# A gated mix of 32-head attention and SwiGLU: K and Q fetched later in each step, one V tile inside the score loop, three gate buffers, an end tile by tile

## The chip, the cores and the metric

One NeuronCore of a Trainium2 chip runs the kernel. The metric is the device time of one execution in microseconds (us), the median over runs. The profile is of one execution on that core.

## The reference

The inputs are x (1, 2048, 512), wqkv (512, 1536), wo (512, 512), w1 and w3 (512, 1792), w2 (1792, 512) and gate_w (512), all float32.

```python
g = sigmoid((x * gate_w).sum(-1, keepdims=True))
q, k, v = split(x @ wqkv)                      # 32 heads of 16
o = softmax(q @ k.T * 16 ** -0.5) @ v          # every query sees every key
a = o @ wo
b = (silu(x @ w1) * (x @ w3)) @ w2
return g * a + (1 - g) * b
```

## The kernel before

**Sizes.** A token tile is 128 tokens (NT = 16), a token quarter 512 (NB = 4), a feature tile 128 (ND = 4 of the 512 features, NF = 14 of the 1792). Projections and products are done in three terms from a high and a low part of each operand (high times high, high times low, low times high), the names end in H/L or h/l.

**Opening.** x is turned and split (xH, xL), the first 128 features of q and k are projected (`project_qk`), and the 16 tiles of V (`sums_v`: 12 full matmuls each, from xH/xL and the split weights wv). The last three V tiles are summed before, and copied out of their banks behind, a branch on a flag (`row_maxima`, `tc.If`) that all engines pass; its body runs for other inputs only.

**The score loop.** Work is cut into 1024 units: (head pair j, half of the queries, key tile k, quarter of the half gq). A unit is one `score` (two 50-row matmuls side by side, then one exponential on ScalarE, L841, from a score bank S into a buffer p) and its share of `pv` (two units at a time, four 17-column products side by side, L821, into acc). 32 units make a step: one head pair against half of the queries, with K and Q in Kt[i], Qt[i], i = step % 2. `evac` stores acc at a step's end.

**An order string written by hand** sets what TensorE does: Q is a score, F a fill slot, P a `pv` call. `run(n)` is n scores and 3n - 3 fill slots, then n/2 P; the pattern `two` has 8 scores, 15 fill slots and two P groups. All of the rest of the kernel goes through the fill slots: `feed` keeps two lanes, each of which does one matmul on 64 rows (half the contraction) per slot, side by side. A block (a product with what is done at its end) takes, say, 12 slots on one lane and then 12 on the other, on one PSUM bank of three, with a tiny VectorE instruction (`tick`, L793) as handover; `pick` hands blocks out in the order of `blocks()` once a bank has rested.

**The blocks in order:** q and k of the remaining features (chunks 0 to 2; `qk_done` splits and stores to qH_d, qL_d, kH_d, kL_d); gate and up for the 14 feature tiles f and four quarters b (chunks 3 to 16; `gate_done` copies to gs, an exponential goes to a buffer `sg`, L460, a reciprocal in eight parts, L463, the product L481 with the up side, and the store of sg to h_d, L482); then h times w2 per token tile in three parts (`h_product`, `load_piece(t, q)` fetches pieces of h and splits them on POOL); then o times wo (`o_product`, `part_product`). w2 takes the place of x, quarter by quarter, once the last chunk is through with that quarter.

**Events by unit number.** At unit 6 of a step, `load_step` fetches K and Q of the next step: 14 transfers on SP's queue, which is worked off in order. `splits`, `soon`, `small`, `later`, `loads` and `stages` are lists from which one or more actions are taken at a score. `divide` normalises finished heads (from D_d, O_d to N_d) and `six_heads` those of the last step.

**Buffers.** Eight exponential buffers p0 to p7, and in the first 512 units four more: od, yy and two halves of bt. In wk lie p, u, od, yy, bt, wo2, wo3; slots `sg` and `gs` have two buffers, `raw` and `fr` three.

**The end.** After the last PV, what is left of the blocks is fed, the last two heads are normalised and turned back, the last feature tile of o (k = 3) is multiplied by wo for token tiles 8 to 14 and all four for tile 15, and each tile is mixed (`mix`, L650) and stored. Tiles 8 and 9, 10 and 11, 12 and 13 are done in pairs; 8 and 10 go over ScalarE (`scaled`, L940) and POOL (L941).

Of the kernel before, what the change touches and what calls it, by code (L numbers as in the profile page):

```python
# [17 lines left out]
P = 128  # L18
# [10 lines left out]
SCALE = DH ** -0.5  # L29
SAFE = 64.0  # L30


@with_exitstack
def gated_mix_kernel(ctx: ExitStack, tc: tile.TileContext, x, wqkv, wo, w1, w3, w2, gate_w, out):
# [28 lines left out]
    fw = ctx.enter_context(tc.tile_pool(name="fw", bufs=2, side="right"))  # L63
    fk = ctx.enter_context(tc.tile_pool(name="fk", bufs=2, side="right"))
    ph1 = ExitStack()
    p1 = ph1.enter_context(tc.tile_pool(name="p1", bufs=1, side="right"))
    wvp = ph1.enter_context(tc.tile_pool(name="wvp", bufs=1))

# [141 lines left out]
    def load_v():  # L210
        for k in range(ND):
            r = slot(("fh1", "fl1", "fh3", "fl3")[k], F32)
            nc.sync.dma_start(r, wqkv[P * k:P * k + P, 2 * D:3 * D])
            vh, vl = (wvp.tile([P, 512], F32R, name=f"v{n}{k}") for n in "hl")
            nc.gpsimd.tensor_copy(vh, r)
            nc.gpsimd.tensor_sub(vl, r, vh)
            wv.append((vh, vl))
# [193 lines left out]
    small = nc.values_load(flag, min_val=0, max_val=1)  # L411
    last_v = [sums_v(t) for t in range(NT - 3, NT)]
    row_maxima(small)
# [38 lines left out]
    def gate_done(f, b):  # L452
        def done(ps):
            gs = slot("gs", F32)
            nc.vector.tensor_copy(gs, ps)  # L455
            sg = slot("sg", F32)
            st = state[b] = dict(gs=gs, sg=sg, exp=False, up=None, gone=False, last=f == NF - 1 or f == NF - 2 and b > 1)

            def exp():
                nc.scalar.activation(sg, gs, AF.Exp, scale=-1.0)  # L460
# [73 lines left out]
    def load_wo(k):  # L534
        if k < 2:
            hi, lo = w2H[3][:, 2 + k, :], w2L[3][:, 2 + k, :]
        else:
            both = wk.tile([P, 2, 512], F32R, name=f"wo{k}")
# [68 lines left out]
    def divide(k, half):  # L607

        yield from reciprocals(k, half)
        for b in (2 * half, 2 * half + 1):  # L610
            for _ in range(5):
                yield
            if half == 0 and k < 3:
                o, r = slot("hx", F32), slot("gw", F32)
            else:
                both = wk.tile([P, 2, 512], F32, name="od")
                o, r = both[:, 0, :], both[:, 1, :]
# [11 lines left out]
    def load_bt(t):  # L629
        if t == 0:  # L630
            bt[-1] = wk.tile([P, 4, 512], F32, name="bt")
        bt[t] = bt[-1][:, t % 3, :]
        nc.sync.dma_start(bt[t], B_d[P * t:P * t + P, :])
# [61 lines left out]
    def six_heads():  # L695
# [8 lines left out]
        nc.sync.dma_start(rows(R_d), dd[rr])  # L704
        both = wk.tile([P, 2, 512], F32, name="od")
        pairs = [(both[:, 0, :], both[:, 1, :]), (slot("fr", F32), slot("sg", F32))]
# [7 lines left out]
        for b in (2, 3):  # L714
# [27 lines left out]
    NBLOCK = 8 * len(chunks) + 3 * NT + NT // 2 + NT // 2  # L742
    source = blocks()

    REST, GAP = 7, 6
    lanes, ready, over = [None, None], ([], []), []
    halves = [None, None]
    tick = const.tile([1, P], F32, name="tick")
# [6 lines left out]
    def pick(lane, rest, gap):  # L755
        if ready[lane] and (ready[lane][0]["since"] + gap <= clock or gap == 0):
            return ready[lane].pop(0)
        used = len(over) - 3
        if used < 0 or over[used] is not None and over[used] + rest <= clock:
            block, halves[lane] = halves[lane] or next(source, None), None  # L760
            if block:
                if type(block[1]) is tuple:
                    product, done, length = block
                    block, halves[1 - lane] = (product, done[0], length), (product, done[1], length)
                over.append(None)
                return dict(block=block, ps=bank(), id=len(over) - 1, n=0, turn=None, alone=halves[1 - lane] is not None or len(over) == NBLOCK)
        return None
# [60 lines left out]
    def score(j, half, k, gq):  # L828
# [7 lines left out]
        n = free.pop(0)  # L836
        if n in ("b0", "b1"):
            p = twin[:, 0:2, :] if n == "b0" else twin[:, 2:4, :]
        else:
            p = wk.tile([P, 2, 512], F32, name=f"p{n}" if type(n) is int else n)  # L840
        nc.scalar.activation(p, ps, AF.Exp, scale=SCALE)  # L841
# [13 lines left out]
    twin = wk.tile([P, 4, 512], F32, name="bt")  # L855

    units = iter([(j, half, k, gq) for half in range(2) for j in range(NPAIR) for k in range(NT) for gq in range(2)])
    pend, clock = [], 0
    for i, c in enumerate(order):
        clock += 1 if c != "P" else 4  # L860
        if c == "Q":
            step = issued // 32 + 1
            if issued % 32 == 6 and step < 2 * NPAIR:
                assert 8 * (ND - 1) - qk_left >= 8 * min(step // 4, ND - 1)
                load_step(step)
# [10 lines left out]
            if small or later and hurry:  # L876
                for _ in range(3 if hurry else 1 + (len(small) > (6 if len(over) < 8 * len(chunks) - 16 else 0))):
                    if small or later and hurry:
                        (small or later).pop(0)()
            if loads and (hurry or issued % 2 or len(over) > 8 * len(chunks) - 12):  # L880
                loads.pop(0)()
# [43 lines left out]
    project(last, 0, (1, 2))  # L925
    project(last, 1, (0, 1))
    rr = slice(PAD, P)
# [10 lines left out]
    def scaled(t):  # L938
        y = wk.tile([P, 512], F32, name=f"p{free[t // 2 - 3]}")
        nc.scalar.activation(y, banks[t], AF.Copy, scale=g[:, t:t + 1])  # L940
        nc.gpsimd.tensor_add(bt[t], bt[t], y)  # L941

    def store(t):
        nc.sync.dma_start(out[P * t:P * t + P, :], bt[t])

    banks[8], banks[9] = one_[:, 1, :], two_[:, 1, :]
    banks[10], banks[11] = bank(), bank()
    for two in ((8, 9), (10, 11), (12, 13), (14,), (15,)):
        if two[0] == 12:
            banks[12], banks[13], banks[14] = psum2()[:, 0, :], psum2()[:, 0, :], acc  # L950
        for terms in ((0, 1), (2,)):
            for t in two:
                project(t, k, terms)
        for t in two:
            if t in (8, 10):
                scaled(t)
            elif t < last:
                mix(t, banks[t], nc.scalar if t % 2 == 0 else nc.sync)
                if t in (9, 11):
                    store(t - 1)  # L960
            else:
                mix(t, banks[t], nc.scalar, slice(0, D // 2))
                mix(t, banks[t], nc.sync, slice(D // 2, D))

# [26 lines left out]
```

## Time and profile before

| what | value |
|---|---|
| median of 3 runs | 1421.45 us (1420.95 to 1421.45) |
| the profiled execution: time, span | 1420.64 us, 1418.8 us |
| busy: TensorE / ScalarE / VectorE / POOL | 1398.6 / 1034.0 / 483.9 / 327.8 us |
| granted TensorE clock, mean | 0.994 |
| moved by DMA | 141.03 MB, mean 99 GB/s |

In a row of the profile stand the line of the kernel, the engine, what was written from what, and how often; in brackets the engine's idle time just before and what ended it. PE is TensorE's matmuls, ACT ScalarE, DVE VectorE, POOL GpSimd; SPq and ACTq are the queues on which transfers are issued. The chain of waits lists the work that ended last in order of time (start, length, what). A table by stretch gives each engine's busy time, then the granted clock, the share of the DMA engines and GB/s.

### The profile page before, as it was taken

How to read it: one execution, taken by the hardware profiler on the slowest of the kernel's cores; microseconds unless marked ns; L12 is line 12 of the kernel's file. 1: busy time of each engine (PE TensorE's matmuls, PEld its weight loads, DVE VectorE, ACT ScalarE, POOL GpSimd, SP SyncE). 2: the span in 40 equal slices, each digit the busy share in tenths (PEclk: the TensorE clock that was granted, in tenths of full speed). 3: DMA queues.
4: the chain of work that ended last, by engine and by line, in shares of the span. 5: the costliest groups of instructions: out<-in, count | busy, mean ns of one | idle time of the engine just before them, and what ended most of it. 6: DMA issues, size and time to landing. Idle time of an engine off the chain costs nothing.

```text
span 1418.8 us, 29039 instructions
## 1 busy us (share of the span) xinstructions
PE 1398.6 (99%) x11497; PEld 835.1 (59%) x11497; DVE 483.9 (34%) x1083; ACT 1034.0 (73%) x1155; POOL 327.8 (23%) x366
## 2 busy tenths in 40 slices
PE   9999999999999999999998999899999999999998
PEld 8875656565656565656564655555555555555554
DVE  5511112554555554655563546210111100111113
ACT  4456767777877777777775777667788878887784
POOL 6114442101001110011101145322333232312312
PEclk9999999999999999999999999999999999999999
DMA  7654554343214333224333165413554543434632
GB/s 207 166 113 108 143 133 104 70 113 69 63 40 98 98 84 68 55 65 110 69 68 69 57 159 120 102 50 83 113 124 91 119 109 76 110 86 108 157 124 77
DMA packets 112479, 141.03 MB, mean 99 GB/s; under 512 B 16276, under 2 KB 70804, under 8 KB 109264
## 3 DMA queue, kind: packets, MB, share of 16 engines
q1 hardware_dynamic: 111616, 137.92, 40.4%
q8 instruction: 93, 1.52, 0.5%
q10 hardware_dynamic: 720, 1.18, 0.2%
q14 instruction: 50, 0.41, 0.1%
HBM read 90.43 MB, written 48.61 MB: 98 GB/s over the span
## 4 chain that ended last, share of the span: by engine, by line
PE 88%; issue 4%; DMA 2%; POOL 2%; SPq 1%; DVE 1%; ACT 1%; DVEq 0%; POOLq 0%; ACTq 0%
PE acc L821 30%; PE f L432 22%; PE S L834 17%; PE f L550 11%; PE f L638 2%; PE S L199 2%; PE f L645 1%; PE f L96 1%; PE f L98 1%; PE f L97 1%; DMA kH_d<-sg 1%; POOL gs L445 1%; DMA h_d<-sg 1%; SPq L270 1%; ACT p L841 1%
## 5 line engine op out<-in xcount | busy, mean ns | idle before, releaser
L841 ACT ACTIVATE p<-S 128x1024 f32<-128x1024 f32 x854 | 810.3, 1026 | 251.1 <-PE S L834 242.0
L834 PE MATMUL S<-Qt,Kt 50*128 50x512 f32 x2048 | 410.3, 407 | 6.1 <-ACT p L841 5.4
L821 PE MATMUL acc<-p,V 128*17 128x512 f32 x3416 | 401.5, 596 | 0.0
L834 PEld LDWEIGHTS S<-Qt,Kt 50*128 50x128 f32 x2048 | 188.3, 185 | 172.9 <-ACT p L841 82.8
L463 DVE RECIPROCAL sg<-sg 128x64 f32<-128x64 f32 x448 | 209.6, 517 | 61.1 <-issue 58.2
L432 PE MATMUL f<-xH,fl 64*128 64x512 f32 x1088 | 224.3, 397 | 0.5 <-DVE tick L793 0.3
L432 PE MATMUL f<-xL,fh 64*128 64x512 f32 x1088 | 222.4, 394 | 0.0
L821 PEld LDWEIGHTS acc<-p,V 128*17 128x17 f32 x3416 | 86.2, 97 | 231.1 <-issue 231.1
L432 PE MATMUL f<-xH,fh 64*128 64x512 f32 x1088 | 221.4, 390 | 0.3 <-DVE gs L455 0.3
L328 POOL CAST fh<-fr 128x512 fp32r<-128x512 f32 x34 | 21.3, 626 | 443.1 <-DMA fr<-in_B_w_dram 358.4
L432 PEld LDWEIGHTS f<-xH,fh 64*128 64x128 f32 x1088 | 108.8, 185 | 24.6 <-DVE gs L455 0.7
L432 PEld LDWEIGHTS f<-xH,fl 64*128 64x128 f32 x1088 | 109.0, 187 | 23.0 <-DVE tick L793 0.8
L432 PEld LDWEIGHTS f<-xL,fh 64*128 64x128 f32 x1088 | 109.0, 187 | 20.9
L793 DVE MEMSET tick<- 1x1 f32 x198 | 11.7, 59 | 306.3 <-PE f L550 181.0
L841 ACT ACTIVATE bt<-S 128x1024 f32<-128x1024 f32 x84 | 82.2, 1028 | 20.3 <-PE S L834 20.3
L841 ACT ACTIVATE od<-S 128x1024 f32<-128x1024 f32 x43 | 44.3, 1029 | 41.4 <-PE S L834 41.4
L550 PE MATMUL f<-xH,fh 64*128 64x512 f32 x208 | 58.3, 394 | 0.0
L550 PE MATMUL f<-xH,fr 64*128 64x512 f32 x160 | 52.0, 397 | 5.9 <-POOL fr L513 5.4
L550 PE MATMUL f<-xH,raw 64*128 64x512 f32 x192 | 57.7, 392 | 0.0
L455 DVE COPY gs<-f 128x512 f32<-128x512 f32 x56 | 38.1, 681 | 55.8 <-PE f L432 53.4
L803 DVE COPY u<-acc 128x512 f32<-128x512 f32 x31 | 21.4, 692 | 104.6 <-PE acc L821 97.1
L550 PE MATMUL f<-xL,fh 64*128 64x512 f32 x208 | 56.1, 392 | 0.0
(211 smaller groups left out, 1577.9 us busy)
## 6 DMA issues: line engine op xcount, KB each, us to landing
Kt<-kH_d SPq DMA_DIRECT2D x128, 128.0 KB
h_d<-sg SPq DMA_DIRECT2D x56, 256.0 KB
sg<-h_d SPq DMA_DIRECT2D x43, 256.0 KB
fr<-in_B_w_dram SPq DMA_DIRECT2D x42, 256.0 KB
Qt<-qH_d SPq DMA_DIRECT2D x128, 64.0 KB
Kt<-kL_d SPq DMA_DIRECT2D x64, 128.0 KB
Qt<-qL_d SPq DMA_DIRECT2D x64, 64.0 KB
b_d<-yy SPq DMA_DIRECT2D x16, 256.0 KB
```

The costliest lines, as they stand in the source:

```text
L96: nc.tensor.matmul(ps, sH, mH, start=first, stop=False)
L199: nc.tensor.matmul(ps[:, i, :], w[i][h][:, k, :], xs[b][:, k, :], start=n == 0, stop=n == len(order) - 1)
L328: nc.gpsimd.tensor_copy(hi, src)
L432: return nc.tensor.matmul(ps, w[i == 1][r, k, :], (xL if i == 2 else xH)[b][r, k, :], start=n == 0 and not second, stop=n == 3 * ND - 1 an ...
L455: nc.vector.tensor_copy(gs, ps)
L463: small.append(lambda q=q: nc.vector.reciprocal(sg[:, q:q + 64], sg[:, q:q + 64]))
L550: ins = nc.tensor.matmul(ps, hs[t][q][i == 1][r, P * o:P * o + P], (w2L if i == 2 else w2H)[q][r, o, :], start=n == 0 and not second, stop ...
L638: return nc.tensor.matmul(ps, ot[t][i == 1][r, P * k:P * k + P], wo_[k][i == 2][r, :], start=n == 0 and not second, stop=n == 3 * ND - 1 a ...
L803: nc.vector.tensor_copy(u, acc)
L821: nc.tensor.matmul(acc[r:r + DH + 1, :], V[:, k, 2 * j + h, :], p[:, h, :], start=k == 0, stop=k == NT - 1)
L834: nc.tensor.matmul(ps[:, h, :], Kt[i][r:r + 50, P * k:P * k + P], Qt[i][r:r + 50, t:t + 512], start=True, stop=True)
L841: nc.scalar.activation(p, ps, AF.Exp, scale=SCALE)
```

## The change

1. `EARLY = 15`: only V tiles 13 and 14 are summed before the loop; tile 15 is the first block of `blocks()`.
2. V's weights move to the pool wvp, kept to the end, as four tiles v0 to v3 of two halves. These are the four extra p buffers (`MORE`), free only when the first run's PV are issued, and later hold od (v2), the third and fourth part of wo and the first pieces of h (v0, v1), and two of the three bt buffers (v3).
3. A third `sg` buffer in wk serves every third gate.
4. `load_step` comes at unit 14 of a step, for units 608 to 639 at 18 of the step, from 640 on at 6.
5. The order string: the first step is 8, 12, 12 instead of 12, 10, 10; 20 run(8) instead of 18 and 43 `two` instead of 45.
6. The last two chunks go through quarters 0, 1, 2 of the last but one, then of the last, then quarter 3 of each, instead of 0 and 1, then 2, then 3.
7. Token tile 13's part of o, like 14's, is two half blocks on two banks without handover; near the end a bank rests 3 instead of 7.
8. The end goes tile by tile, all mixed on VectorE.

```diff
+EARLY = 15
+    wvp = ctx.enter_context(tc.tile_pool(name="wvp", bufs=1))
     p1 = ph1.enter_context(tc.tile_pool(name="p1", bufs=1, side="right"))
-    wvp = ph1.enter_context(tc.tile_pool(name="wvp", bufs=1))
...
-            vh, vl = (wvp.tile([P, 512], F32R, name=f"v{n}{k}") for n in "hl")
+            both = wvp.tile([P, 2, 512], F32R, name=f"v{k}")
+            vh, vl = both[:, 0, :], both[:, 1, :]
...
-    last_v = [sums_v(t) for t in range(NT - 3, NT)]
+    last_v = [sums_v(t) for t in range(13, EARLY)]
...
-            sg = slot("sg", F32)
+            sg = wk.tile([P, 512], F32, name="sg") if (NB * f + b) % 3 == 2 else slot("sg", F32)
...
-            both = wk.tile([P, 2, 512], F32R, name=f"wo{2 + q}")
+            both = wvp.tile([P, 2, 512], F32R, name=f"v{q}")
...
-        turns += [(last - i, b) for two in ((0, 1), (2,), (3,)) for i in (1, 0) for b in two]
+        turns += [(last - i, b) for some in ((0, 1, 2), (3,)) for i in (1, 0) for b in some]
+        for t in range(EARLY, NT):
+            yield v_product(t), v_done(t), 3 * ND
...
+    def v_product(t):
+        b, o = divmod(P * t, 512)
+        def product(ps, r, n, second):
+            k, i = divmod(n, 3)
+            return nc.tensor.matmul(ps, (xL if i == 1 else xH)[b][r, k, o:o + P], wv[k][i == 2][r, :],
+                                    start=n == 0 and not second, stop=n == 3 * ND - 1 and second)
+        return product
+
+    def v_done(t):
+        return lambda ps: nc.vector.tensor_copy(V[:, t, :, 0:DH], ps.rearrange("p (h d) -> p h d", d=DH))
...
-        for t in range(NT // 2, NT - 2):
+        for t in range(NT // 2, NT - 3):
             yield part_product(t, True), part_done(t), LATE
-        yield part_product(NT - 2, False), (part_done(NT - 2), part_done(NT - 2)), LATE
+        for t in (NT - 3, NT - 2):
+            yield part_product(t, False), (part_done(t), part_done(t)), LATE
...
-        if used < 0 or over[used] is not None and over[used] + rest <= clock:
+        if used < 0 or over[used] is not None and over[used] + (rest if len(over) < NBLOCK - 3 else 3) <= clock:
...
-    THIRDS, LONG, SHORT = 16, 18, 45
+    THIRDS, LONG, SHORT = 16, 20, 43
-    order = (run(12) + run(10) * 2) * THIRDS + run(8) * LONG + "QQ" + "F" * 7 + two * SHORT + "QFFF" * 5 + "QPPPP"
-    MORE = ["od", "yy", "b0", "b1"]
-    free = list(range(NP)) + MORE
+    order = run(8) + run(12) * 2 + (run(12) + run(10) * 2) * (THIRDS - 1) + run(8) * LONG + "QQ" + "F" * 7 + two * SHORT + "QFFF" * 5 + "QPPPP"
+    MORE = ["v0", "v1", "v2", "v3"]
+    free = list(range(NP))
...
-            if issued % 32 == 6 and step < 2 * NPAIR:
+            if issued % 32 == (14 if issued < 608 else 18 if issued < 640 else 6) and step < 2 * NPAIR:
...
+            if issued == 8 and not pend:
+                free += MORE
...
-    project(last, 1, (0, 1))
+    project(last, 1)
...
-    project(last, 1, (2,))
-    project(last, 2)
+    project(last, 2, (0, 1))
...
-    for two in ((8, 9), (10, 11), (12, 13), (14,), (15,)):
...
+    project(8, k, (0, 1))
+    project(last, 2, (2,))
+    project(8, k, (2,))
+    mix(8, banks[8])
+    for t in range(9, NT):
...
+        project(t, k)
+        if t < last:
+            mix(t, banks[t], nc.scalar if t % 2 else nc.sync)
```

More of the change, by code (lines that the diff above doesn't have):

```diff
@@ L537, in load_wo @@
         else:
-            both = wk.tile([P, 2, 512], F32R, name=f"wo{k}")
+            both = wvp.tile([P, 2, 512], F32R, name=f"v{k - 2}")
             hi, lo = both[:, 0, :], both[:, 1, :]
@@ L615, in divide @@
             else:
-                both = wk.tile([P, 2, 512], F32, name="od")
+                both = wvp.tile([P, 2, 512], F32, name="v2")
                 o, r = both[:, 0, :], both[:, 1, :]
@@ L630, in load_bt @@
         if t == 0:
-            bt[-1] = wk.tile([P, 4, 512], F32, name="bt")
-        bt[t] = bt[-1][:, t % 3, :]
+            both = wvp.tile([P, 2, 512], F32, name="v3")
+            bt[-3], bt[-2] = both[:, 0, :], both[:, 1, :]
+            bt[-1] = wk.tile([P, 512], F32, name="bt")[:]
+        bt[t] = bt[t - 3]
         nc.sync.dma_start(bt[t], B_d[P * t:P * t + P, :])
@@ L704, in six_heads @@
         nc.sync.dma_start(rows(R_d), dd[rr])
-        both = wk.tile([P, 2, 512], F32, name="od")
+        both = wvp.tile([P, 2, 512], F32, name="v2")
         pairs = [(both[:, 0, :], both[:, 1, :]), (slot("fr", F32), slot("sg", F32))]
@@ L736, in blocks @@
             yield o_product(t), o_done(t), 3 * ND
-        for t in range(NT // 2, NT - 2):
+        for t in range(NT // 2, NT - 3):
             yield part_product(t, True), part_done(t), LATE
-        yield part_product(NT - 2, False), (part_done(NT - 2), part_done(NT - 2)), LATE
+        for t in (NT - 3, NT - 2):
+            yield part_product(t, False), (part_done(t), part_done(t)), LATE
     LATE = 3 * (ND - 1)
-    NBLOCK = 8 * len(chunks) + 3 * NT + NT // 2 + NT // 2
+    FIRST = NT - EARLY + 8 * len(chunks)
+    NBLOCK = FIRST + 3 * NT + NT // 2 + NT // 2 + 1
     source = blocks()
@@ L746, in gated_mix_kernel @@
     lanes, ready, over = [None, None], ([], []), []
-    halves = [None, None]
+    halves = [[], []]
     tick = const.tile([1, P], F32, name="tick")
@@ L758, in pick @@
         used = len(over) - 3
-        if used < 0 or over[used] is not None and over[used] + rest <= clock:
-            block, halves[lane] = halves[lane] or next(source, None), None
+        if used < 0 or over[used] is not None and over[used] + (rest if len(over) < NBLOCK - 3 else 3) <= clock:
+            alone = bool(halves[lane])
+            block = halves[lane].pop(0) if alone else next(source, None)
             if block:
@@ L763, in pick @@
                     product, done, length = block
-                    block, halves[1 - lane] = (product, done[0], length), (product, done[1], length)
+                    block, alone = (product, done[0], length), True
+                    halves[1 - lane].append((product, done[1], length))
                 over.append(None)
-                return dict(block=block, ps=bank(), id=len(over) - 1, n=0, turn=None, alone=halves[1 - lane] is not None or len(over) == NBLOCK)
+                return dict(block=block, ps=bank(), id=len(over) - 1, n=0, turn=None, alone=alone)
         return None
@@ L836, in score @@
         n = free.pop(0)
[L837 to L840, printed above, removed]
+        p = (wk if type(n) is int else wvp).tile([P, 2, 512], F32, name=f"p{n}" if type(n) is int else n)
         nc.scalar.activation(p, ps, AF.Exp, scale=SCALE)
@@ L848, in gated_mix_kernel @@
     NP = 8
-    THIRDS, LONG, SHORT = 16, 18, 45
+    THIRDS, LONG, SHORT = 16, 20, 43
     run = lambda n: "QQFFFFFF" + "QFFF" * (n - 3) + "Q" + "P" * (n // 2)
     two = "QFFF" * 5 + "QPPQQPP"
-    order = (run(12) + run(10) * 2) * THIRDS + run(8) * LONG + "QQ" + "F" * 7 + two * SHORT + "QFFF" * 5 + "QPPPP"
-    MORE = ["od", "yy", "b0", "b1"]
-    free = list(range(NP)) + MORE
-    twin = wk.tile([P, 4, 512], F32, name="bt")
+    order = run(8) + run(12) * 2 + (run(12) + run(10) * 2) * (THIRDS - 1) + run(8) * LONG + "QQ" + "F" * 7 + two * SHORT + "QFFF" * 5 + "QPPPP"
+    MORE = ["v0", "v1", "v2", "v3"]
+    free = list(range(NP))
     units = iter([(j, half, k, gq) for half in range(2) for j in range(NPAIR) for k in range(NT) for gq in range(2)])
@@ L876, in gated_mix_kernel @@
             if small or later and hurry:
-                for _ in range(3 if hurry else 1 + (len(small) > (6 if len(over) < 8 * len(chunks) - 16 else 0))):
+                for _ in range(3 if hurry else 1 + (len(small) > (6 if len(over) < FIRST - 16 else 0))):
                     if small or later and hurry:
                         (small or later).pop(0)()
-            if loads and (hurry or issued % 2 or len(over) > 8 * len(chunks) - 12):
+            if loads and (hurry or issued % 2 or len(over) > FIRST - 12):
                 loads.pop(0)()
@@ L934, in gated_mix_kernel @@
         nc.vector.tensor_sub(Ol[k][rr, a, :], back[a][rr, :], Oh[k][rr, a, :])
-    project(last, 1, (2,))
-    project(last, 2)
[L938 to L944, printed above, removed]
+    project(last, 2, (0, 1))
     banks[8], banks[9] = one_[:, 1, :], two_[:, 1, :]
     banks[10], banks[11] = bank(), bank()
-    for two in ((8, 9), (10, 11), (12, 13), (14,), (15,)):
-        if two[0] == 12:
-            banks[12], banks[13], banks[14] = psum2()[:, 0, :], psum2()[:, 0, :], acc
[L951 to L963, printed above, removed]
+    project(8, k, (0, 1))
[3 more added lines that the diff above has]
+    for t in range(9, NT):
+        if t == 12:
+            banks[12], banks[13], banks[14] = psum2()[:, 0, :], psum2()[:, 0, :], acc
+        project(t, k)
+        if t < last:
+            mix(t, banks[t], nc.scalar if t % 2 else nc.sync)
+        else:
+            mix(t, banks[t], nc.scalar, slice(0, D // 2))
+            mix(t, banks[t], nc.sync, slice(D // 2, D))
 _INS = ['A_x', 'A_wqkv', 'A_wo', 'B_w1', 'B_w3', 'B_w2', 'gate_w']
```

## The prediction

> **What bounds the kernel now.** I read the page first: the engine that is nearly always busy sets the time, if it is busy at full clock.
>
> ```profile
> PE 1398.6 (99%) x11497; PEld 835.1 (59%) x11497; DVE 483.9 (34%) x1083; ACT 1034.0 (73%) x1155; POOL 327.8 (23%) x366
> ```
>
> TensorE it is: only its work, its order and its stops count. The stops show in the chain of waits in order of time, where each run of scores and fill ends in one group of PV products (L821): the distance between two such groups is the length of a run.
>
> ```profile
> 220.28 5.28 PE acc L821 x48
> ...
> 262.67 5.27 PE acc L821 x48
> ...
> 757.99 4.42 PE acc L821 x40
> ...
> 787.50 3.56 PE acc L821 x32
> 798.00 3.56 PE acc L821 x32
> ...
> 903.28 3.56 PE acc L821 x32
> ...
> 933.55 3.56 PE acc L821 x32
> ...
> 1107.57 1.84 PE acc L821 x16
> ...
> 1117.00 1.84 PE acc L821 x16
> ```
>
> A step of 32 units (runs of 12, 10, 10) takes 42.39 us, run(8) 10.50, the pattern `two` (also 8 units) 9.43. Against that, 757.99 to 787.50 is 29.51, where two runs of 8 and the longer first PV group (4.42 - 3.56) make 21.86: **7.65 us lost**. 903.28 to 933.55 is 30.27 for two runs: **9.27 lost**. Then the rows of TensorE, ScalarE, SP's queue and the wait list, for what ended each stop:
>
> ```profile
> 780.11 0.79 PE L834 MATMUL S<-Qt,Kt 50*128 50x512 f32 x2 [5.12 <-ACT p L841]
> ```
> ```profile
> 778.51 0.63 ACT L460 ACTIVATE sg<-gs 128x512 f32<-128x512 f32 x1 [7.50 <-DMA h_d<-sg]
> ```
> ```profile
> 766.15 0.36 SPq L277 DMA_DIRECT2D Qt<-qH_d  x1
> ...
> 773.30 10.16 SPq L482 DMA_DIRECT2D h_d<-sg  x2
> ```
> ```profile
> 773.30 5.13 DMA h_d<-sg
> ```
> ```profile
> ACT sg L460 <- DMA h_d<-sg: 18.1, 4, 7.5
> ```
>
> First stop, read backwards: a score waits for a score bank, which ScalarE empties; ScalarE stands 7.50 us before a gate's exponential, whose `sg` buffer (two, in turn) is still being stored to h_d; that store came to the head of SP's queue at 773.30, behind the 14 transfers of the `load_step` begun at 766.15, and took 5.13. ScalarE waits so four times, 18.1 us in all; the other three cost TensorE little.
>
> ```profile
> 905.88 0.45 SPq L277 DMA_DIRECT2D Qt<-qH_d  x1
> ...
> 913.49 7.83 SPq L512 DMA_DIRECT2D sg<-h_d  x4
> ```
> ```profile
> 918.49 0.79 PE L550 MATMUL f<-xH,fr 64*128 64x512 f32 x1 [5.39 <-POOL fr L513]
> ```
>
> Second stop, same queue: the pieces of h for token tile 1 (`load_piece(1, 2)`, `(1, 3)`, into `fr`) sit behind a `load_step` that holds SP from 905.88 to 913.4; TensorE waits 5.39 for their split.
>
> **The change, part by part.** Its sum stands against this execution: 1418.8 us of span, 1420.64 of time, so 1.84 around the span; the median of the runs, 1421.45, is 0.8 above it.
>
> *Third `sg` buffer, `load_step` at unit 14.* A gate-up pair takes 24 fill slots; at 87 slots per 42.39 us that is 11.7, so the buffer written now was last taken two pairs ago (23.4 us), with three buffers 35.1. ScalarE was 7.50 short; 11.7 more leaves 4.2 over. The fetch still holds SP for 773.30 - 766.15 = 7.15 us, whatever its unit: moved from 6 to 14 it goes behind the qk stores, chunk weights, h stores and (unit 12) `dd` loads issued in between, and ahead of those after. At 14 it no longer follows the accumulator's eight stores directly. Queued behind it is now the h store of that moment, for which ScalarE waits two buffers later: covered by the 4.2. For the first stop I take -7.6 (bounds -7.6 and 0: no row shows three buffers; the nearest, the 7.50, is exceeded by 11.7). Small losses: 16 steps of 42.39 from the first score, 81.40 (row below), would end at 759.64, and the sixteenth ends at 757.99 + 4.42 = 762.41, 2.8 late. I take 1.5 of it as gone, the rest as the qk part's own, where `gs` and slot `sg` stay two (bounds 0 and -2.8).
>
> *Unit 18 for units 608 to 639.* I walked both order strings, counting slots. Before, the fetch stands at unit 614 and the pieces (1, 2), (1, 3) at 615 and 616. After, the pieces stand at 620 and 621, the fetch at 626; they are first used at slot 1711, unit 634, a run after they are asked for. The last product of the last chunk is 5 units later (619): its gate now ends inside the run of units 608 to 615, so its exponential comes at 616, not 608; its store feeds token tiles 12 to 15 alone. -9.3 (bounds -9.3, 0). What is late next: the last two pieces of w2 come at units 614 and 615 instead of 612 and 613, and are used from slot 1673, unit 619. One PV group, 3.56, lies between and covers the transfer. I put +0.5 there, from 0 to 3.6 (that cover gone). The fetch of step 20 keeps 14 units, 18 us at 10.50 per 8.
>
> *Order and V tile 15.*
>
> ```profile
> 80.06 0.39 PE L97 MATMUL f<-vl,xH 128*128 128x512 f32 x1
> 80.29 0.39 PE L98 MATMUL f<-vh,xL 128*128 128x512 f32 x1
> 81.40 0.93 PE L834 MATMUL S<-Qt,Kt 50*128 50x512 f32 x4 [0.72 <-DVE V L415]
> ```
> ```profile
> 73.76 0.55 SPq L282 DMA_DIRECT2D Qt<-m_d  x2
> 79.75 0.32 SPq L277 DMA_DIRECT2D Qt<-qH_d  x1
> ```
>
> Tile 15 was 12 full matmuls at a pitch of 0.23: 2.7 us. As a block it is 24 half matmuls, two side by side, 12 slots. Two `two` (15 slots each) become two run(8) (21 each), exactly those 12: 2 x (10.50 - 9.43) = +2.1. The first step's order 8, 12, 12 has the same number of runs and slots. In return the first score could come 2.7 earlier, at 78.7; but SP, which must pass the If too, issues nothing between 73.76 and 79.75. I take the first score at 80.1, -1.3 (bounds -2.7, 0; nearest is SP's row). [...] The buffers v0 to v3 hold V's weights until the block's last slot, 27; their first exponential is the ninth of the second run, near slot 48: no wait. The copy of V's tile on VectorE is the same copy, moved (34% busy). Without that cover a wait there would be one copy, below 1 us.
>
> *3 and 1 token quarters; buffers.* The same blocks in another order; w2's first pieces move from unit 560 to 574, the first pieces of h from 564 to 580, both far ahead of the first h product (slot 1633, unit 604): 0. `od`, `wo2`, `wo3` and most of `bt` move to v0 to v3 with the same lifetimes: 0. If this cover failed, it would be a stop as at 918.49.
>
> *End.*
>
> ```profile
> 1403.03 0.50 PE L645 MATMUL f<-wo,xL 64*128 64x512 f32 x1
> 1403.37 0.39 PE L645 MATMUL f<-wo,xH 64*128 64x512 f32 x1
> ```
> ```profile
> 1409.81 0.37 SPq L651 DMA_DIRECT2D out_dram<-xH  x1
> 1410.93 0.36 SPq L944 DMA_DIRECT2D out_dram<-xH  x1
> ```
> ```profile
> GB/s 0 0 0 0 0 0 0 191 410 355 210 0 200 410 364 383 401 337 392 346 419 364 382 401 346 392 410 346 373 373 364 341 355 328 132 0 0 0 0 0
> ```
>
> Tile 13 without turns saves a handover and adds one sum on VectorE, hidden in PV; by the slot count three fill slots are left behind the last PV group, two before: +0.3. Then the same matmuls, tile by tile. The last row is 1409 to 1418 in columns of 0.225 us: the first output tile flows for 0.7, then a hole of 0.4, since tiles 8 and 9, 10 and 11 are finished in pairs and two of them pass ScalarE and POOL; then the bus is full for 5 us to 1416.8. Tile by tile the first store leaves three matmuls (0.69) sooner and 0.3 later for the fill slot, near 1409.4, and each next 0.69 after it, which is what a tile takes on the bus: no hole, nothing heaped up, the end set by the last half tile's store, whose product comes as late as now. -1.0 (bounds -1.4, 0).
>
> **Sum:** -7.6 - 1.5 - 9.3 + 0.5 + 2.1 - 1.3 + 0.3 - 1.0 = -17.8; 1420.64 - 17.8 = 1402.8. The median stands up to 0.8 higher: I say **1403**.
>
> **Rivals.** *A, the second stop moves:* the last w2 or h pieces are late after all. For it: w2's last piece now queues behind an h piece on POOL, which splits in order. Against it: the half run and more between each asking and use. 3 to 9 of the 9.27 us back: 1406 to 1412. *B, the clock.*
>
> ```profile
> 772.85:787.50 14.65, 9.53 (x66) 7.12 (x66) 6.00 (x17) 7.29 (x8) 0.00 (x0) 0.77 0.36 65
> ```
>
> Around the first stop the granted clock averaged 0.77, and of the 7.65 lost only 5.12 were idle: 2.5 went to matmuls at the lower clock. Now TensorE idles before the first score from the end of tile 14, 81.40 - 2.7 - 0.7 = 78.0, to 80.1: 2.1 us where it was 0.72. If that lowers the clock: +2.5, 1405.5. [...] *C, the store still holds ScalarE* (fetch, stores and weights heaped at unit 14): the 7.6 stay: 1410.5. *D, slower:* K and Q come late. After unit 14, 18 of 32 units are left, 23.8 us; the fetch takes 7.2 to issue, and a transfer lands 5.13 later, so 11.5 are over. Only if the last landed 11.5 + 1 us late at each of some 19 step boundaries would the 18 us be eaten: above 1421.5. No wait for Kt is among the stops now. *E:* the stops have another cause: 1421.
>
> **How the numbers follow.** Forecast 0.70 (1399.5 to 1406), A 0.12, B 0.07, C 0.05, D 0.04, E 0.02. A change under 0.2% (2.8 us) is about what measuring this kernel can't tell from none: faster 0.94, same 0.02, slower 0.04. Low end, every bound at its best: -7.6 - 2.8 - 9.3 + 2.1 - 2.7 + 0.3 - 1.4 = -21.4, 1399.3. High end: into A, 1409, which leaves out half of A, C, D and E, under 2 in 10.
>
> **What would show it.** No row of L460 waiting for h_d longer than 1 us, 757.99 to 787.50 shrunk to 22; no `fr` wait near unit 620; first score near 80; 43 pairs of short PV groups instead of 45; outputs flowing without a hole. I am wrong if a TensorE gap above 3 us is left between the first score and 1390, first of all on w2 or h pieces, or at a step's first score on Kt.

## The result, and the profile after

The changed kernel takes 1405.42 us in the median of 5 runs (1404.03 to 1406.1), the kernel before beside it 1420.95 (1420.15 to 1421.45): a ratio of 0.9892, 95% interval 0.9881 to 0.9903. The profiled execution took 1406.1 us with a span of 1404.3, so 14.5 us of span are gone. The forecast was 1403, in a range of 1399.3 to 1409.0.

Busy rows of the engines, changed kernel:

```profile
PE 1394.3 (99%) x11509; PEld 834.9 (59%) x11509; DVE 486.6 (35%) x1086; ACT 1031.6 (73%) x1153; POOL 325.9 (23%) x364
```

TensorE still sets the time. The chain of waits in order of time, at the places of the two big stops (start, length, what; the PV products are L842 here, the gate's exponential L462, scores L855):

```profile
769.66 3.56 PE acc L842 x32
780.17 3.56 PE acc L842 x32
790.68 3.56 PE acc L842 x32
...
895.71 3.56 PE acc L842 x32
906.34 3.56 PE acc L842 x32
916.88 3.56 PE acc L842 x32
927.42 3.56 PE acc L842 x32
```

769.66 to 790.68 is 21.02 for two runs of 8, 906.34 to 927.42 is 21.08: both stops are gone to the last half microsecond. Between the last V product and the last PV, TensorE still idles in three places, in brackets in its rows; the one ahead of the first score is longer than before (2.16 us against 0.72):

```profile
77.53 0.39 PE L99 MATMUL f<-v,xL 128*128 128x512 f32 x1
80.08 0.93 PE L855 MATMUL S<-Qt,Kt 50*128 50x512 f32 x4 [2.16 <-SPq L295]
...
118.75 0.50 PE L434 MATMUL f<-xH,fl 64*128 64x512 f32 x2 [0.89 <-DVE tick L814]
...
191.12 0.49 PE L434 MATMUL f<-xH,fl 64*128 64x512 f32 x2 [0.70 <-DVE tick L814]
```

And the granted clock falls where it did not fall before (stretch, its length, then each engine's busy time with the count, the granted clock, DMA share, GB/s):

```profile
78.40:81.81 3.41, 1.73 (x15) 1.58 (x16) 0.25 (x1) 0.87 (x1) 0.00 (x0) 1.00 0.04 12
81.81:85.23 3.42, 3.42 (x20) 2.91 (x18) 0.00 (x0) 2.34 (x4) 0.00 (x0) 0.50 0.00 0
85.23:88.64 3.41, 3.41 (x32) 2.66 (x32) 0.12 (x2) 3.34 (x4) 0.00 (x0) 1.00 0.00 0
```

20 matmuls fall into the half-clock stretch, 32 into the next one.

To see where the time went I took off from each run, of the length that the chain gives it, what it needs by itself: 0.2325 us for each score and fill slot, 0.2 for the switch, and its PV group (5.28, 4.42, 3.56 or 1.84); these are worked out from the 42.39, 10.50 and 9.43 us of before and add up to them. The rest is what the run lost:

| stretch of the score loop | lost before, us | lost after, us |
|---|---|---|
| first run | 0.06 | 1.56 |
| runs 2 to 12 (q and k blocks) | 0.92 | 1.99 |
| runs 13 to 48 | 1.76 | 0.80 |
| the runs of 8 (both big stops) | 17.39 | 0.50 |
| the pattern `two` | -0.47 | +0.42 |

That is 14.4 less; the order costs 2.1 more (two run(8) for two `two`), the first score comes 1.3 earlier, and from the last PV's end to the span's end it takes 14.75 us instead of 15.7: 14.4 - 2.1 + 1.3 + 0.95 = 14.5.

### The profile page after: what moved, and what is told of

It is laid out like the page before. It is cut to its first block, busy times and chain, and to the rows that moved or that the text cites. A ratio compares the mean times of both kernels' runs of the same rounds, so it can differ in the third digit from the quotient of the medians.

```text
span 1404.3 us, 29060 instructions
## 1 busy us (share of the span) xinstructions
PE 1394.3 (99%) x11509; PEld 834.9 (59%) x11509; DVE 486.6 (35%) x1086; ACT 1031.6 (73%) x1153; POOL 325.9 (23%) x364
## 3 DMA queue, kind: packets, MB, share of 16 engines
q10 hardware_dynamic: 864, 1.44, 0.3%
## 4 chain that ended last, share of the span: by engine, by line
PE 87%; issue 3%; POOL 1%; DMA 0%; DVE 0%; DVEq 0%; POOLq 0%
PE acc L842 31%; PE f L434 24%; PE S L855 18%; PE f L552 11%; PE f L642 2%; PE f L649 1%; POOL gs L447 1%; POOL sg L446 0%; PE f L926 0%; DMA qL_d<-gs 0%; PE S L926 0%; POOL fl L331 0%; DVE xL L654 0%; POOL fh L330 0%; DVE gs L445 0%
## 5 line engine op out<-in xcount | busy, mean ns | idle before, releaser
L855 PE MATMUL S<-Qt,Kt 50*128 50x512 f32 x2048 | 411.9, 408 | 2.2 <-SPq L295 2.2
L842 PE MATMUL acc<-p,V 128*17 128x512 f32 x3424 | 400.1, 594 | 0.0
L855 PEld LDWEIGHTS S<-Qt,Kt 50*128 50x128 f32 x2048 | 188.9, 185 | 170.9 <-ACT p L859 77.4
L434 PE MATMUL f<-xH,fl 64*128 64x512 f32 x1088 | 225.3, 396 | 1.6 <-DVE tick L814 1.6
L434 PE MATMUL f<-xL,fh 64*128 64x512 f32 x1088 | 223.8, 393 | 0.0
L842 PEld LDWEIGHTS acc<-p,V 128*17 128x17 f32 x3424 | 86.2, 97 | 229.3 <-issue 229.3
L434 PE MATMUL f<-xH,fh 64*128 64x512 f32 x1088 | 222.0, 389 | 0.0
L859 ACT ACTIVATE v<-S 128x1024 f32<-128x1024 f32 x168 | 160.7, 1028 | 55.3 <-PE S L855 55.1
L814 DVE MEMSET tick<- 1x1 f32 x198 | 11.7, 59 | 290.4 <-PE f L552 144.6
L842 PE MATMUL acc<-v,V 128*17 128x512 f32 x672 | 80.9, 593 | 0.0
L552 PE MATMUL f<-xH,fl 64*128 64x512 f32 x208 | 64.8, 392 | 0.0
L552 PE MATMUL f<-xL,fh 64*128 64x512 f32 x208 | 63.4, 392 | 0.0
L552 PE MATMUL f<-xH,raw 64*128 64x512 f32 x192 | 62.9, 392 | 0.0
L552 PE MATMUL f<-xH,fh 64*128 64x512 f32 x208 | 60.9, 392 | 0.0
L573 DVE SCALAR_TENSOR_TENSOR yy<-f,omg,yy 128x512 f32<-128x512 f32 x32 | 24.0, 751 | 102.5 <-PE f L552 102.5
```

The lines of the kernel that those rows point to most:

```text
L434: return nc.tensor.matmul(ps, w[i == 1][r, k, :], (xL if i == 2 else xH)[b][r, k, :], start=n == 0 and not second, stop=n == 3 * ND - 1 an ...
L552: ins = nc.tensor.matmul(ps, hs[t][q][i == 1][r, P * o:P * o + P], (w2L if i == 2 else w2H)[q][r, o, :], start=n == 0 and not second, stop ...
L573: nc.vector.scalar_tensor_tensor(y, ps, omg[:, t:t + 1], y, op0=OP.mult, op1=OP.add)
L842: nc.tensor.matmul(acc[r:r + DH + 1, :], V[:, k, 2 * j + h, :], p[:, h, :], start=k == 0, stop=k == NT - 1)
L855: nc.tensor.matmul(ps[:, h, :], Kt[i][r:r + 50, P * k:P * k + P], Qt[i][r:r + 50, t:t + 512], start=True, stop=True)
```

## The experiments

### What removed the two stops: buffer, place of the fetch, or order?

**Two `sg` buffers again.**

```diff
-            sg = wk.tile([P, 512], F32, name="sg") if (NB * f + b) % 3 == 2 else slot("sg", F32)
+            sg = slot("sg", F32)
```

> The changed kernel with two sg buffers again for every gate; the fetch stays at unit 14 (18). Theory: the third buffer is what removed the first stop and about 0.9 us of small losses, so both come back: a row of the gate's exponential (L460) with a wait of 4 to 7.5 us for the store h_d<-sg, a pair of runs of 8 longer than 21 us by 4 to 7.6, and a time 5 to 9 us above the changed kernel's 1405.4, near 1412. Rival 1: the fetch at unit 14 alone cured the stop, since the store then no longer comes behind it at that moment: no wait over 1 us, time within 1.5 us of 1405.4. Rival 2: the stop only moves, to the h store that is now behind the fetch: same 7 us, other place.

Measured: 1403.96 us (1403.56 to 1406.19), ratio to before 0.9884 (0.9870 to 0.9898), against 0.9892 of the whole change. No stop came back. So the third buffer isn't needed in this kernel, and my argument for the first stop rested on it.

**The kernel before with the fetch's line alone.**

```diff
-            if issued % 32 == 6 and step < 2 * NPAIR:
+            if issued % 32 == (14 if issued < 608 else 18 if issued < 640 else 6) and step < 2 * NPAIR:
```

> The kernel before with one line of the change alone: the fetch of K and Q at unit 14 of a step, at 18 for units 608 to 639, at 6 from 640 on. After the run with two sg buffers (no stop came back) the theory is: the place of the fetch on SP's queue is what removes both stops, 7.65 and 9.27 us: 1404 us, within 2 us of the whole change, and neither the third buffer, the order of quarters, V tile 15 nor the end adds anything that shows. Rival 1: the second stop needs the new order of quarters too, since before the pieces of h and the group's store come later: 1409 to 1413, a stop of 5 to 9 us at 906. Rival 2: the first stop needs more than the fetch in the old order: a wait of ScalarE for the store of h_d near 772, 1411.

Measured: 1406.25 us (1405.22 to 1407.53), ratio 0.9902 (0.9886 to 0.9917). One line has 14.3 of the 15.5 us; the 0.8 us between this kernel and the changed one lie inside the two intervals. In its chain neither place has a stop (the longest run here is 0.4 us over its length):

```profile
770.54 3.56 PE acc L821 x32
781.06 3.56 PE acc L821 x32
791.57 3.56 PE acc L821 x32
...
896.85 3.56 PE acc L821 x32
907.73 3.57 PE acc L821 x32
918.24 3.56 PE acc L821 x32
928.74 3.56 PE acc L821 x32
```

and SP's queue shows why at the first: the two stores of `sg` go out ahead of the fetch, where before they came to the head of the queue behind it.

```profile
770.52 8.05 SPq L482 DMA_DIRECT2D h_d<-sg  x2
778.66 0.61 SPq L595 DMA_DIRECT2D dd<-d_d  x1
779.33 0.47 SPq L277 DMA_DIRECT2D Qt<-qH_d  x1
```

ScalarE's wait for a store to h_d, 7.50 us before, is one of 0.8 in the whole execution.

**The same with unit 14 below 608 and 6 from there on.**

```diff
+            if issued % 32 == (14 if issued < 608 else 6) and step < 2 * NPAIR:
```

> The kernel before with the fetch at unit 14 for units below 608, at 6 from there on (no 18): half of the line that gave 14.3 us by itself. Theory: the two halves are independent, one stop each: the first stop goes (-7.6 us, with up to 1 more from the smaller waits), the second stays with 9 us, 1412.5; and the 18 for units 608 to 639 is worth the other 6 to 9. Rival: with the first stop gone the second is another one (the clock's fall and the store's delay before it are gone too), and most of it goes: 1407.

Measured: 1415.27 us (1413.04 to 1415.89). The runs of 8 lose 9.73 us in all, 9.22 of it in one pair:

```profile
897.66 3.56 PE acc L821 x32
915.89 5.05 PE acc L821 x32
```

TensorE's wait there is again the split of an h piece (`PE f L550 <- POOL fr L513`, 5.7 us once). So the two halves of the line are independent: unit 14 takes the first stop (1420.9 to 1415.3; 7.6 less the 2.0 that runs 2 to 12 lose by it, below), unit 18 for 608 to 639 takes the second, 1415.27 - 1406.25 = 9.0.

**The changed kernel with that fetch back at unit 614.**

```diff
-            if issued % 32 == (14 if issued < 608 else 18 if issued < 640 else 6) and step < 2 * NPAIR:
+            if issued % 32 == (14 if issued < 608 else 6) and step < 2 * NPAIR:
```

> The changed kernel with the fetch at unit 6 of the step for units 608 to 639 (unit 614) instead of 18; from there on as before, and unit 14 below 608 as in the change. Theory of the prediction: the place of this one fetch is what removed the second stop, so a wait of up to 9.3 us comes back between the group of the last chunk and the second token tile: 1410 to 1415. Rival: the new order of the last two chunks, and 12 more slots, put the w2 and h pieces far enough ahead by themselves: with the fetch at 614 only w2 pieces 12 and 13 (asked at 614 and 615, used from 619) come behind it. That covers: within 1.5 us of 1405.4. Middle case: w2's last piece late, a stop of 1 to 5 us at unit 619 to 621 that waits for a split on POOL.

Measured: 1410.17 us (1409.18 to 1410.69), 4.8 above the changed kernel: the middle case. One run loses 4.92. Its rows, TensorE, POOL and SP's queue:

```profile
905.11 0.56 PE L552 MATMUL f<-xH,fh 64*128 64x512 f32 x1 [2.73 <-POOL xH L515]
```
```profile
904.44 0.61 POOL L515 CAST xH<-fr 128x512 fp32r<-128x512 f32 x1 [5.80 <-DMA fr<-in_B_w_dram]
```
```profile
892.88 0.45 SPq L279 DMA_DIRECT2D Qt<-qH_d  x1
...
899.23 0.36 SPq L514 DMA_DIRECT2D fr<-in_B_w_dram  x1
```

The last piece of w2, asked for one unit behind the fetch, is issued at 899.23, when the 14 transfers are through, and TensorE is there before its split. The h pieces, which made the stop before, are no longer the ones that are late. In the new order the fetch's place is worth about half of what it is in the old one.

**Fetch back at unit 6 for 512 to 607, with three and with two `sg` buffers.**

```diff
-            if issued % 32 == (14 if issued < 608 else 18 if issued < 640 else 6) and step < 2 * NPAIR:
+            if issued % 32 == (14 if issued < 512 else 6 if issued < 608 else 18 if issued < 640 else 6) and step < 2 * NPAIR:
```

The second kernel has the first experiment's line as well.

> The changed kernel, three sg buffers, with the fetch of steps 17 to 19 back at unit 6 (units 518, 550, 582), at 18 for units 608 to 639 as in the change. Theory of the prediction: the third buffer alone gives ScalarE 11.7 us more, so no wait of L462 for the store to h_d over 1 us and no stop near 772: 1405.4 within 1. Rival: the third buffer does not help, as the store behind the fetch is later than that, or another resource behind the fetch (the next h store, a weight chunk) stops TensorE instead: a stop of 4 to 8 us near 772, 1409 to 1413.

> As the kernel beside it (fetch at 518, 550, 582), but with two sg buffers for every gate. Theory: the first stop of the kernel before is back, a wait of 5 to 7.5 us of L462 for h_d<-sg at 770 to 780 and 7 us more, 1412. Rival: the new order (runs of 8, 12, 12; gates 12 slots later in the units) has shifted the gates past the fetch by itself, so neither buffer nor fetch is needed: 1405.4.

Measured: 1405.42 us (1403.98 to 1405.53) and 1404.58 (1404.32 to 1405.33). Neither stops near 772, not even with two buffers and the fetch where it was before. ScalarE's rows show why. First the kernel before, whose next exponential is the row at 778.51 with its 7.50 us of waiting (shown in the prediction); then two buffers with the fetch at 6 in the new order; then the kernel of a later experiment, with V tile 15 ahead of the branch again:

```profile
770.39 0.62 ACT L460 ACTIVATE sg<-gs 128x512 f32<-128x512 f32 x1
```
```profile
770.88 0.62 ACT L462 ACTIVATE sg<-gs 128x512 f32<-128x512 f32 x1
781.40 0.62 ACT L462 ACTIVATE sg<-gs 128x512 f32<-128x512 f32 x1
```
```profile
769.28 1.14 ACT L462 ACTIVATE sg<-gs 128x512 f32<-128x512 f32 x2
```

In the old order two gates became due at the same run's end, 770.39 and right behind it (778.51 - 7.50 = 771.0); the second needs the buffer whose store hangs behind the fetch. With V tile 15's 12 slots in front, every gate ends 12 slots later, and near this place one exponential falls to each run's end, 10.5 us apart; with tile 15 ahead of the branch the two come together again. So the first stop has two cures here, each enough: the fetch behind the stores, shown by its line alone, or the new order, by these rows through its shift of the gates. Whether the third buffer is a third cure was not tried: it would need the kernel with tile 15 ahead of the branch, where the two gates come together, with the fetch back at unit 6.

### The clock after the first gap

**14 transposes ahead of the branch.**

```diff
+    idle(14)
     row_maxima(small)
```

> The changed kernel with 14 transposes of the identity (0.11 us each, 1.5 us) behind the last V product and ahead of the branch, so that TensorE idles about 0.6 us instead of 2.16 before the first score. Theory: the idle time is what dropped the granted clock to half from 81.81 to 85.23: here no half clock before the end, the first run 1.5 us shorter, 1403.9. Rival 1: the drop has another cause (the score loop's beginning itself): half clock at the same place, 1405.4. Rival 2: the branch begins later by the transposes' time and so does the first score (TensorE, not SP, is last through it): up to 1.5 us later, so no gain.

Measured: 1405.64 us (1405.14 to 1405.89), no gain, and yet the first run loses 0.11 us instead of 1.56 and there is no half clock until the end. Rival 2 took it back. The branch (L295), as the queues saw it, in the changed kernel and with the transposes (duration in ns, start in us):

```profile
L295 SPq EVENT_SEMAPHORE  x8: 17/17/17, 79.0 to 79.5; - x8
...
L295 PEldq COMPARE_BRANCH  x1: 5639/5639/5639, 73.7 to 73.7; - x1
L295 SPq COMPARE_BRANCH  x1: 50/50/50, 75.7 to 75.7; - x1
```
```profile
L295 SPq COMPARE_BRANCH  x1: 50/50/50, 74.9 to 74.9; - x1
L295 PEldq COMPARE_BRANCH  x1: 3374/3374/3374, 76.5 to 76.5; - x1
```

In the changed kernel SP is the last one through the branch, if only just: its last semaphore row starts at 79.5, TensorE's branch row ends at 79.3 (73.7 + 5.64), and the first score's row names SPq L295. With the transposes TensorE's sequencer comes to the branch 1.6 us after SP, its row there is 3.37 us long, and it is the last:

```profile
80.66 0.73 PE L856 MATMUL S<-Qt,Kt 50*128 50x512 f32 x3 [1.54 <-PEq L295]
```

The first score comes 5.8 us after SP's branch (80.66 - 74.9) instead of 4.4 (80.08 - 75.7). 1.4 lost there, 1.45 won by the clock. Half the transposes might win something; that wasn't tried.

### V tile 15

**Ahead of the branch again.**

```diff
-EARLY = 15
+EARLY = 16
-    THIRDS, LONG, SHORT = 16, 20, 43
+    THIRDS, LONG, SHORT = 16, 18, 45
-    order = run(8) + run(12) * 2 + (run(12) + run(10) * 2) * (THIRDS - 1) + run(8) * LONG + ...
+    order = (run(12) + run(10) * 2) * THIRDS + run(8) * LONG + ...
-    free = list(range(NP))
+    free = list(range(NP)) + MORE
...
-            if issued == 8 and not pend:
-                free += MORE
```

> The changed kernel with V tile 15 summed before the branch again, the first step as runs of 12, 10, 10, 18 runs of 8 and 45 of the pattern two; everything else of the change stays. Theory: V tile 15 inside the loop cost 2.1 us of order and 1.5 us of low clock and brought 1.3 us at the first score: first score at 81.4, no half clock at 82 to 85, time 2.3 us lower, 1403.1. Rival 1: the drop of the clock is not tied to the idle time: 0.8 lower, 1404.6. Rival 2: the 12 slots also moved the qk part's blocks, and the two new stops there (108 and 183 us) belong to that: they go too, 2 us more, 1401.

Measured: 1408.94 us (1407.22 to 1412.08), slower than the changed kernel. The first run loses 0.10 and the first score is at 80.32, but one run of 8 loses 6.42: the fetch at unit 590 stands in front of a w2 piece, and the pieces of h queue behind that on POOL.

```profile
870.32 0.42 SPq L279 DMA_DIRECT2D Qt<-qH_d  x1
...
877.60 0.36 SPq L514 DMA_DIRECT2D fr<-in_B_w_dram  x1
```
```profile
PE f L552 <- POOL fh L515: 2.5, 1, 2.5
```

**The same with that one fetch at unit 582.**

```diff
-            if issued % 32 == (14 if issued < 608 else 18 if issued < 640 else 6) and step < 2 * NPAIR:
+            if issued % 32 == (14 if issued < 576 else 6 if issued < 608 else 18 if issued < 640 else 6) and step < 2 * NPAIR:
```

> The run with V tile 15 ahead of the branch again, with the one fetch that ran into the w2 and h pieces there (unit 590) moved to unit 582. Theory: its stop of 6.4 us at 877 to 894 goes, and what is left is the price of V tile 15 inside the loop, 2.1 us of order less 0 to 1.3 us of first score: 1402.5 to 1404.5, against 1405.4 of the changed kernel. Rival 1: the stop stays, because the pieces are late for another reason (POOL, the transfers of w2 themselves): 1408.9. Rival 2: V tile 15 in the loop is worth nothing, one way or the other: 1405.4 within 0.7.

Measured: 1406.15 us, but 1404.26 to 1409.99 over five runs: inconclusive against 1405.4. The stop shrinks from 6.42 to 2.03 and does not go. What holds it now is POOL: it idles 4.70 us up to 865.45, and from there to 887.1 its splits of w2 and h stand back to back, some 1.9 us each, while TensorE, whose first h product comes at 878.75 instead of 881.34, waits for those of h near their end. In the changed kernel POOL is through with what it has at 872.59 and waits 7.47 us for w2. So a block moved by 12 slots here meets another alignment of units and slots, and its price of 2.1 us cannot be read apart from that. What tile 15 is worth, with POOL's and SP's work arranged for either place, stays open.

### The small stops of the q and k part

**A third `gs` buffer there** (the tile `bt`, unused until the end).

```diff
+    n_qk = 0
...
-            lo = slot("gs", F32)
+            nonlocal n_qk
+            n_qk += 1
+            lo = slot("gs", F32) if n_qk % 3 else wk.tile([P, 512], F32, name="bt")
```

> The changed kernel with a third gs buffer for every third q/k block of the loop's first part (the bt buffer, free until the end). Theory: the two small stops at 118 and 191 us (1.16 and 0.93 us over the runs' own length; 1.0 to 3.6 in the other kernels) come from VectorE's copy into gs, which waits for the store of the block two before, with the handover between the lanes queued behind it: both gone, 2 us less, 1403.4, and no half clock after 118. Rival: VectorE waits for POOL's split or for the sg slots (still two) instead: the stops stay, 1405.4.

Measured: 1402.5 us (1402.48 to 1403.77), ratio 0.9874 (0.9859 to 0.9889); none of its runs is above the fastest of the changed kernel's (1404.03). Runs 2 to 12 lose -0.15 us instead of 1.99. VectorE's waits with a store behind them from 85 to 230 us, in the changed kernel and here (waiting instruction, what for: total, times, longest):

```profile
DVE gs L445 <- PE S L855: 7.8, 3, 3.2
DVE gs L445 <- DMA qL_d<-gs: 5.6, 2, 3.1
DVE gs L445 <- DMA kL_d<-gs: 1.7, 1, 1.7
```
```profile
DVE gs L449 <- DMA kL_d<-gs: 1.5, 1, 1.5
DVE bt L449 <- DMA kH_d<-sg: 1.5, 1, 1.5
```

And VectorE's rows ahead of the stop at 118.75 in the changed kernel:

```profile
114.07 0.69 DVE L445 COPY gs<-f 128x512 f32<-128x512 f32 x1 [1.67 <-DMA kL_d<-gs]
118.01 0.69 DVE L445 COPY gs<-f 128x512 f32<-128x512 f32 x1 [3.25 <-PE S L855]
118.64 0.06 DVE L814 MEMSET tick<- 1x1 f32 x1
```

The copy at 118.01 waits for its buffer, the handover (L814) stands behind it on VectorE, and TensorE behind the handover. (The rows with `PE S L855` name a score, which was done long before; I read them as waits for a store, here that of qL_d, which left SP's queue at 114.48. That they go with the third buffer bears this out.) The stop is the fetch's doing: the kernel before with the fetch's line alone has it too, 1.44 and 1.06 us in the runs where before it lost 0.40 and 0.56. At unit 14 the 14 transfers run into the stores of the q and k blocks. The loss in runs 2 to 12 varies: 2.0 to 2.8 us in six traces with V tile 15 in the loop and two `gs` buffers, 4.6 in a seventh (two `sg` buffers), where the clock fell too.

### The end

**The changed kernel with the end in pairs.** The edit puts back the old text from `project(last, 1, ...)` on, with `scaled` and `store`.

```diff
...
-    for t in range(9, NT):
+    for two in ((8, 9), (10, 11), (12, 13), (14,), (15,)):
...
```

> The changed kernel with the end in pairs again, tiles 8 and 10 over ScalarE and POOL; the three half blocks stay. Theory: the end is 1.0 us longer: last PV to the end 15.8 us instead of 14.8, a hole of 0.4 us in the outgoing bytes, 1406.4. Rival: the outgoing transfers end when the last product's store ends, whatever the order before it: 14.8 and 1405.4.

Measured: 1406.24 us (1406.21 to 1406.35). The last PV ends at 1388.72, the span at 1404.4: 15.7 us, against 14.75 tile by tile: 0.95 us, where the theory said 1.0. The first stores of both kernels on SP's queue, tile by tile first:

```profile
1395.76 1.68 SPq L655 DMA_DIRECT2D out_dram<-xH  x2
```
```profile
1395.65 0.37 SPq L655 DMA_DIRECT2D out_dram<-xH  x1
```

From the last PV's end to the first store it takes 6.2 us tile by tile (1395.76 - 1389.55) and 6.9 in pairs (1395.65 - 1388.72).

### Together

**Third `gs` and transposes.** The two edits above in one kernel.

> The changed kernel with the third gs buffer and the 14 transposes ahead of the branch: no small stops at 118 and 191, and never half clock behind the first score. Theory: 1402.5 or up to 0.7 lower, since the third-gs kernel lost 1.5 us to the clock in some of its runs, and here it can lose it in none; no run above 1403. Rival: the transposes hold the first score back by as much as the clock costs on average: 1402.5 to 1403.5.

Measured: 1403.25 us (1402.97 to 1406.34). The profiled execution keeps the full clock to the end and loses nothing in the q and k part, but its first score is at 80.71. Of the other executions one, at 1406.34, has a granted clock of 0.998; what happened in it is not known. So the rival holds: no gain over the third buffer alone. The fastest version of this study is the changed kernel with the third `gs` buffer alone, 1402.5 us.

## Why the prediction came out as it did

**Right.** The sum foretold a span 17.8 us shorter; it is 14.5. The two stops bring what they were to bring: 16.9 us in the runs of 8, foretold -7.6 - 9.3. The order costs 2.1 as counted. The first score came at 80.08 (foretold 80.1), because SP is, by 0.2 us, the last through the branch; among the seven kernels with this opening, the changed one with them, it lies between 78.83 and 80.67, so that hit is luck by half a microsecond. That SP's passage would not move with TensorE's work, on which the -1.3 stands, no row of before shows; in the runs SP's branch row begins at 75.6 before and 75.7 after, though TensorE's begins 2.8 us earlier (76.5, then 73.7). The end: the tile-by-tile part was put at -1.0 and measures 0.9; the third fill slot at 1390.06 is there, and the foretold +0.3 for it does not show, -0.95 in all against -0.7. (The low end of the range adds up to 1399.2, not 1399.3.)

**Wrong in the cause: "Third `sg` buffer".** I gave the first stop's 7.6 us to the buffer and treated the fetch's place as neutral ("still holds SP", 7.15 us, "whatever its unit"). It holds SP as long, but what stands behind it is another transfer; the line alone cures the stop with two buffers. Nor did I see that the 12 slots move the gates to one per run, which cures it too, though I had walked the order string for the second stop. The size came out right because every cure removes the same 7.65; that is luck, and no run shows what the third buffer would bring by itself.

**"Unit 18 for units 608 to 639": right.** Back at 614 the time is 4.8 higher, not 9.3, since the new order already frees the h pieces, and w2's last piece is late next, as the text named it. The +0.5 for it did not come: no wait on w2 in the changed kernel.

**"Small losses", -1.5: mis-sized, wrong sign in one part.** Runs 13 to 48 gained 0.96. Runs 2 to 12 lost 1.07 more: I had written that the q and k part keeps its losses because `gs` and `sg` stay two, and did not follow the moved fetch past the q and k stores, though I listed them as what it goes behind. Net +0.1 instead of -1.5.

**Rival B came beside the forecast, not in its place.** I gave the clock 0.07 and 2.5 us. In the profiled execution it fell, 1.5 us in the first run. Of the other kernels with this opening and no transposes it fell there with the fetch back at unit 614 (0.67 from 78 to 82) and with the third `gs` buffer (0.50 from 81.73 to 85.14), and not with two `sg` buffers (1.00 from 78 to 90) nor with the end in pairs (1.0 over the whole execution). That rival B's time, 1405.5, is next to the measured one is chance: the fall cost less than its 2.5, and the small losses made up the rest. The 0.07 was my estimate; the stretches ahead of the two falls inside the loop of the kernel before were idle by 0.94 and 1.00, and nothing there shows that 2.1 us would keep the clock. The gap of 2.16 us was enough.

**Left over:** the pattern `two` lost 0.9 more over 86 repetitions, 0.01 each; the same figure is -0.42 to -0.48 in five of the kernels here and +0.3 to +0.9 in the other nine, with no part of the change that goes along with it, and I have no cause for it. 1.5 (clock) + 1.6 (small losses) + 0.9 - 0.5 - 0.25 = 3.3 is what the span came out above the sum.

## What to carry to other kernels

On a queue that is worked off in order, a long burst of transfers can cost what stands behind it (here 14 transfers held SP's for 7.15 us, and 7.65 were lost behind them): when such a burst is moved, list the transfers that it now holds up as carefully as those it sets free, and who waits for each. Before a stall is credited to a buffer, look at what else in the change moves the writer, the reader or the store of that buffer; several edits can each remove the same stall, and then they don't add up. And filling an engine's idle time ahead of a point that all engines pass can make that engine the last one there (14 transposes: TensorE came to the branch 1.6 us after SP instead of 2.0 before it).

## What the runs showed of the hardware

**In these traces the clock changed on a raster of 3.413 us, and in the changed kernel a stretch idle by 0.49 was enough for a fall.** In the traces of the changed kernel and of the kernel before, the points at which the granted clock changes lie whole multiples of 3.413 us apart (changed: 1402.77 - 81.81 = 1320.96 = 387.0 times; before: 918.15 - 785.03 = 133.12 = 39.0 times, 1416.50 - 924.98 = 491.52 = 144.0 times). A fall went with TensorE's idle share between two such points. In the changed kernel the stretch ahead of the fall, 78.40 to 81.81, is idle by 0.49 (1.73 busy of 3.41). With two `sg` buffers the gap ahead of the first score was longer, 2.36 us, but fell across a point, and the clock held; later it fell after 1.56 us within one stretch:

```profile
75.79:79.20 3.41, 2.52 (x12) 1.74 (x10) 1.38 (x2) 0.00 (x0) 0.00 (x0) 1.00 0.16 24
79.20:82.61 3.41, 1.94 (x15) 1.72 (x16) 0.00 (x0) 1.07 (x2) 0.00 (x0) 1.00 0.04 12
82.61:86.03 3.42, 3.42 (x30) 3.17 (x29) 0.12 (x2) 3.42 (x4) 0.00 (x0) 1.00 0.00 0
116.75:120.16 3.41, 1.85 (x15) 0.80 (x16) 0.69 (x2) 1.64 (x3) 2.74 (x4) 1.00 0.30 88
120.16:123.57 3.41, 3.41 (x20) 0.76 (x16) 0.00 (x0) 0.82 (x1) 2.26 (x3) 0.50 0.43 153
```

Stretches at full clock that were idle by 0.36 (the fetch back at unit 614, 116.92 to 120.33), 0.43 (79.20 above) and 0.45 (the transposes, 77.92 to 81.33) were followed by full clock. From 0.46 to 0.49 it went both ways: 0.46 (116.75 above) and 0.49 (the changed kernel) were followed by half clock, 0.48 (the kernel before, 911.32 to 914.73) by full. After 0.54 (the third `gs` buffer, 78.32 to 81.73), 0.94 and 1.00 (the kernel before, 774.80 to 778.21 and 914.73 to 918.15) it was half. (The transposes count as work in this: without their 1.2 us the stretch with the gap, 77.92 to 81.33, would be idle by 0.8, and it kept the clock.) Once at half, a stretch idle by 0.56 and one idle by only 0.26 (the kernel before, 778.21 to 781.62 and 918.15 to 921.56) were followed by a second one at half, while those without idle time (81.81 in the changed kernel, 781.62 and 921.56 before) were followed by full clock. So nearly the same gap cost 1.5 us in one execution and nothing in another, by where it fell: 2.16 us lost the clock in the changed kernel, 2.36 kept it with two `sg` buffers.

**The branch, passed, took 3.37 to 5.64 us on TensorE's queue and 3.3 to 3.8 on SP's.** TensorE's sequencer's row for it is 3.37 us long with the transposes (76.5 to 79.9) and 3.99 in the kernel before (76.5 to 80.5), where it comes to the branch 1.6 and 0.9 us after SP. In the changed kernel, where it comes there 2.0 us before SP, the row is 5.64 us long. SP's first row behind the branch comes 3.3 us after its branch row in the changed kernel (75.7 to 79.0), 3.5 in the kernel before (75.6 to 79.1) and 3.8 with the transposes (74.9 to 78.7). No run here shows what these times consist of.
